# First unit of weights in two halves ahead of attention, next three units two places sooner

## The chip, the core and the metric

The kernel runs on one core of one Trainium2 chip. A time is the device time of one execution in microseconds (us); three executions of the kernel before took 899.27 us in the median (897.33 to 899.37). The engines are TensorE (PE; its weight loads are shown as PEld), VectorE (DVE), ScalarE (ACT), GpSimd (POOL) and SyncE (SP), which here issues nearly all DMA transfers. Each engine runs its own instructions in their order and waits on semaphores for the others.

## What is computed

Local attention with a few global tokens, and a feed-forward network over its output, in 32-bit floats.

```python
def _attn_ref(q_l, k_l, v_l, q_g, k_g, v_g):          # 8 batches, 8 heads, 512 local + 32 global, 64 wide
    s_g = scale * np.matmul(q_g, k_all.transpose(0, 1, 3, 2))      # global queries see all keys
    out_g = np.matmul(sm(s_g), v_all)
    s_ll = np.where(abs(pos[:, None] - pos[None, :]) <= 32, s_ll, -1e9)
    a_l = sm(np.concatenate([s_lg, s_ll], axis=-1))                # local queries: 32 global + a band
    out_l = np.matmul(a_l, np.concatenate([v_g, v_l], axis=2))
    return np.concatenate([out_g, out_l], axis=2)
def _moe_ref(x, w_in, w_out):                          # 4352 tokens, 512 -> 2048 -> 512
    h = x @ w_in
    g = np.where(h > 0.0, h, np.exp(np.minimum(h, 0.0)) - 1.0)
    return g @ w_out
```

The weights w_in and w_out arrive as 64-bit floats.

## The kernel before

Two streams are written into one program. `attention()` yields some hundreds of places; at each place i it writes the pieces that its plan has for that place: loads (k, q, the global queries qg, v), S (scores on PE, masked and reduced on DVE, line 752, exponentials on ACT, line 757), T (turning p, PE line 774, copies to pt on DVE and ACT, line 777), V (product with v, PE line 803, division on DVE, line 817) and X (the output turned to feature-major, xr). A head group g holds four heads; a tile t is 128 local queries. The first pieces, of batch 0 and group 0, are the scores of the global queries (PE line 705, maximum mg on DVE line 708, exponentials on ACT line 711) and the tiles 0 to 3.

`ffn_stream()` is the feed-forward part. It multiplies in 16 bits, each number split into a high and a low half (win and wout "h" and "l"; x likewise), with scales that are powers of two. Its first matmuls are line 316.

Between the two, `load_weights()` makes these halves from the 64-bit weights, in 16 units of 1 MB: unit 0 is the first part of w_in, unit 1 the first of w_out, and so on in turn. `fetch` loads a unit into a tile `raw`, of which there are two; `unit` then defers its steps to later places:

- s0: ACT takes the absolute value of the high word into `cu` (line 178), POOL clamps it (line 179)
- s1m (w_in only): DVE reduces its maximum (line 183)
- s1a, s1b, s1c: DVE shifts the word and merges sign and low bits into it (lines 187, 190, 194), "the words"; after s1c `raw` is free, and SP's next fetch waits for that
- s1d to s4: scales, and the two 16-bit halves (lines 200, 212 and 215)

Up to place 57 (`lead`) no feed-forward work is written, and `UNITS` names the places at which a unit is taken up; each such call fetches one unit ahead and starts the steps of the one before. From place 49 on `convert` paces the units instead. All steps but s0 and s2 are written "behind", with a priority 60 lower. The scheduler that turns this into each engine's order moves rows by these priorities and by its own model of times, so the order of an engine isn't that of the code.

DMA transfers go out in SP's order. A transfer whose buffer is still in use stops SP, with all that stands behind it.

Of the kernel before, what the change touches and what calls it, by code (L numbers as in the profile page):

```python
# [10 lines left out]
F32 = mybir.dt.float32  # L11
F32R = mybir.dt.float32r
I32 = mybir.dt.int32
AF = mybir.ActivationFunctionType
ALU = mybir.AluOpType
AX = mybir.AxisListType
# [6 lines left out]
P = 128  # L23
# [15 lines left out]
NBL = B * SL // BLK  # L39
GROUPS = {"a": (0, 2), "b": (2, 4), "c": (4, 6), "d": (6, 8), "f": (0, 8)}  # L40
BEHIND = 60
UNITS = 0, 7, 17, 28
NX = 4
TURNED = 4

# [5 lines left out]
FMIN = struct.unpack("f", struct.pack("I", 0x38000000))[0]  # L51
FMAX = struct.unpack("f", struct.pack("I", 0x47efe000))[0]
# [5 lines left out]
def attn_ffn(ctx: ExitStack, tc: tile.TileContext, qT, qgT, kT, vT, w_in, w_out, mask, out):  # L58
    nc = tc.nc
# [75 lines left out]
    w1 = w_in.bitcast(I32).rearrange("(c p) (f w) -> p c f w", p=P, w=2)  # L135
    w2 = w_out.bitcast(I32).rearrange("(f p) (e w) -> p f e w", p=P, w=2)
# [10 lines left out]

    def load_weights():
        todo = [(group, m, p) for group in "abcd" for p in range(*GROUPS[group]) for m in range(2)]
        raws = [fetch(*todo[0][1:])]  # L150
        yield
        for n, (group, m, p) in enumerate(todo):
            if n + 1 < len(todo):
                raws.append(fetch(*todo[n + 1][1:]))
            unit(m, p, raws[n])
            if (m, p) == (1, GROUPS[group][1] - 1):
                defer(12, lambda group=group: tables(group))
                if p == NP - 1:
                    defer(13, lambda: tables("f"))
            yield  # L160

    def fetch(m, p):
        raw = ffn.tile([P, NC, 2 * P, 2] if m == 0 else [P, 2, DM, 2], I32, name="raw")
        nc.sync.dma_start(raw, w1[:, :, 2 * p * P:2 * (p + 1) * P, :] if m == 0 else w2[:, 2 * p:2 * p + 2, :, :])
        return raw

    def unit(m, p, raw):
        f = slice(2 * p * P, 2 * (p + 1) * P)
        shape = [P, NC, 2 * P] if m == 0 else [P, 2, DM]
        parts = [w[:, :, f] for w in win] if m == 0 else [w[:, 2 * p:2 * p + 2, :] for w in wout]  # L170
        pw = (pww if m == 0 else pwo)[:, p:p + 1]
        u = ffn.tile(shape, F32, name="cu", bufs=3)
        mx = ffn.tile([P, 4], F32, name="cm", bufs=4)
        high, low = raw[..., 1], raw[..., 0]
        ui = u.bitcast(I32)

        def s0():
            nc.scalar.activation(u, high.bitcast(F32), AF.Abs)
            nc.gpsimd.tensor_scalar(u, u, FMAX, FMIN, ALU.min, ALU.max)

        def s1m():
            if m == 0:
                nc.vector.tensor_reduce(out=mx[:, 0:1], in_=u, op=ALU.max, axis=AX.XY)

        def s1a():
            tc.keep_in_program_order(
                nc.vector.tensor_scalar(ui, ui, 3, 0x3ffffff8, ALU.logical_shift_left, ALU.bitwise_and))

        def s1b():
            nc.vector.scalar_tensor_tensor(out=ui, in0=high, scalar=-0x40000000, in1=ui,  # L190
                                           op0=ALU.bitwise_and, op1=ALU.bitwise_or)

        def s1c():
            nc.vector.scalar_tensor_tensor(out=ui, in0=low, scalar=29, in1=ui,
                                           op0=ALU.logical_shift_right, op1=ALU.bitwise_or)

        def s1d():
            if m:
                dump = ffn.tile([P, 10, P], F32, name="gx", bufs=1)[:, 0:8, :].rearrange("p (a b) x -> p a (b x)", a=2)
                nc.scalar.activation(dump, u, AF.Abs, accum_out=mx[:, 1:2])  # L200

        def s2():
            if m == 0:
                all_max(mx[:, 1:2], mx[:, 0:1])

        def s3():
            if m:
                power(pw, mx[:, 1:2])
            else:
                power_of_wide(pw, mx[:, 1:2], mx[:, 2:3])  # L210
            inverse(mx[:, 3:4], pw)
            nc.scalar.activation(parts[0], u, AF.Copy, scale=mx[:, 3:4])

        def s4():
            nc.vector.scalar_tensor_tensor(out=parts[1].rearrange("p a b -> p (a b)") if m else parts[1],
                                           in0=u.rearrange("p a b -> p (a b)") if m else u, scalar=mx[:, 3:4],
                                           in1=parts[0].rearrange("p a b -> p (a b)") if m else parts[0],
                                           op0=ALU.mult, op1=ALU.subtract)

        d = 1 if lead[0] else 2  # L220
        lag = 7 if m else 13
        for i, fn in ((1, s0), (1 + d, s1m), (1 + d, s1a), (1 + 2 * d, s1b), (1 + 3 * d, s1c), (1 + 4 * d, s1d),
                      (1 + lag, s2), (2 + lag, s3), (3 + lag, s4)):
            defer(i, (lambda fn=fn: behind(fn)) if fn not in (s0, s2) else fn)

    def tables(group):
# [729 lines left out]
    for i, _ in enumerate(attention()):  # L956
        lead[0] = i < PACE[1][0]
        if i in UNITS:
            next(units)
# [70 lines left out]
```

## Time and profile before

| | us |
|---|---|
| median of three executions | 899.27 |
| the profiled execution | 901.09 |
| its span, first to last instruction | 899.0 |
| busy: PE, DVE, ACT, POOL | 859.6, 686.2, 598.8, 85.9 |
| DVE busy from 10.5 to 62 us | 49.60 of 51.50 |
| PE busy from 200 to 899 us | 685.59 of 699 |

All views come from the one profiled execution. Times in them count from its first instruction, and a row of the view in order of time gives start, duration, engine, line, operation, output and inputs, and in brackets how long the engine had been idle and what ended that. "issue" there is idle time for which the profile shows no cause. A row of the waits gives the total, how often, and the longest. The share of DMA is the mean over 16 DMA engines. Neighbouring instructions on DVE overlap by some hundredths of a microsecond, so that their durations add up to a little more than the time they take.

### The profile page before, as it was taken

Reading aid. Unit: us, or ns where it says so; the run is one execution under the profiler, and the core shown is the slowest. Engines: PE = TensorE matmul, PEld = TensorE weight load, DVE = VectorE, ACT = ScalarE, POOL = GpSimd, SP = SyncE. Lnnn points to the kernel's source line nnn. Section 1 sums busy time; section 2 is a strip of 40 time slices with the busy share of each in tenths; the row PEclk is TensorE's granted clock in tenths of the full one; section 3 lists DMA queues with packets and bytes.
Section 4 is the critical chain, followed back from the end, with each engine's and each line's share of the span. In section 5 each row is a group of like instructions: output and inputs, shape, how many; then the busy total and the mean of one; then the engine's idle time right before and its main releaser. Section 6 shows DMA issues by size and latency. Waiting matters only on the chain.

```text
span 899.0 us, 27480 instructions
## 1 busy us (share of the span) xinstructions
PE 859.6 (96%) x11648; PEld 693.1 (77%) x11648; DVE 686.2 (76%) x1910; ACT 598.8 (67%) x1093; POOL 85.9 (10%) x140
## 2 busy tenths in 40 slices
PE   7779999989999999999999999999999999999997
PEld 4557666656656888888878888888888888888886
DVE  5996999989976768776766768686777677766565
ACT  4758987666665656676756667666667666666564
POOL 1110234213210000000000000000000000020000
PEclk7889999999999999999999999999999999999999
DMA  7975756423463335132341335132431211020000
GB/s 284 338 248 179 246 204 223 155 94 111 163 209 133 96 112 160 50 81 66 103 126 47 96 112 160 51 91 85 134 109 57 56 60 47 25 25 24 1 25 24
DMA packets 64818, 103.68 MB, mean 115 GB/s; under 512 B 31288, under 2 KB 31928, under 8 KB 64696
## 3 DMA queue, kind: packets, MB, share of 16 engines
q1 hardware_dynamic: 64408, 101.66, 35.7%
q8 instruction: 92, 1.51, 0.7%
q14 instruction: 30, 0.25, 0.1%
q10 hardware_dynamic: 288, 0.26, 0.1%
HBM read 80.41 MB, written 15.20 MB: 106 GB/s over the span
## 4 chain that ended last, share of the span: by engine, by line
PE 57%; DVE 24%; ACT 13%; issue 3%; DMA 3%; SPq 0%; DVEq 0%; ACTq 0%
PE pa L316 22%; PE acc L474 10%; PE h L474 8%; DVE gl L337 3%; PE acc L439 3%; PE h L316 3%; ACT p L757 3%; ACT gh L353 2%; PE pa L741 2%; PE pa L774 2%; DVE gx L334 2%; PE pa L803 2%; ACT g L325 2%; ACT hs L326 1%; ACT g L327 1%
## 5 line engine op out<-in xcount | busy, mean ns | idle before, releaser
L316 PE MATMUL pa<-x,winh 128*128 128x256 f16 x1648 | 277.5, 273 | 0.6 <-ACT xglob L847 0.6
L316 PEld LDWEIGHTS <-winh 128*128 128x128 f16 x2160 | 208.2, 98 | 36.0 <-issue 4.2
L316 PE MATMUL pa<-x,winl 128*128 128x256 f16 x824 | 224.6, 273 | 0.0
L353 ACT ACTIVATE gh<-gx,xs 128x896 f16<-128x896 f32 x103 | 107.6, 1045 | 142.9 <-DVE gx L350 142.8
L337 DVE SCALAR_TENSOR_TENSOR gl<-gx,xs,gh 128x896 f16<-128x896 f32 x103 | 118.4, 1149 | 76.1 <-ACT gh L353 75.9
L474 PEld LDWEIGHTS <-gh 128*128 128x128 f16 x1456 | 139.8, 98 | 18.8 <-issue 1.4
L334 DVE SCALAR_TENSOR_TENSOR gx<-g,hs 128x512 f32<-128x512 f32 x103 | 71.1, 690 | 76.3 <-ACT g L327 75.6
L316 PEld LDWEIGHTS <-winl 128*128 128x128 f16 x1080 | 105.9, 98 | 12.9 <-issue 0.2
L757 ACT ACTIVATE p<-p,m 128x128 f32<-128x128 f32 x256 | 81.4, 391 | 28.3 <-DVE m L752 28.3
L316 PE MATMUL h<-x,winh 128*128 128x256 f16 x512 | 88.1, 275 | 0.0
L474 PE MATMUL acc<-wouth,gh 128*128 128x256 f16 x312 | 85.2, 273 | 0.0
L474 PE MATMUL acc<-woutl,gh 128*128 128x256 f16 x312 | 85.1, 273 | 0.0
L474 PE MATMUL acc<-wouth,gl 128*128 128x256 f16 x312 | 85.0, 273 | 0.0
L327 ACT ACTIVATE g<-g 128x512 f32<-128x512 f32 x135 | 84.9, 629 | 0.0
L325 ACT ACTIVATE g<-pa,xs 128x512 f32<-128x512 f32 x103 | 70.1, 680 | 17.5 <-PE pa L316 16.6
L474 PEld LDWEIGHTS <-gl 128*128 128x128 f16 x728 | 71.2, 98 | 9.3 <-DVE gl L337 1.0
L474 PE MATMUL h<-raw,gh 128*128 128x256 f16 x416 | 74.6, 273 | 0.0
L587 POOL TENSOR_SCALAR xs<-isc,xm 128x2 f32<-128x2 f32 (+1 forms) x28 | 19.1, 682 | 566.2 <-DVE xm L115 422.3
L316 PE MATMUL h<-x,winl 128*128 128x256 f16 x256 | 70.2, 275 | 0.0
L326 ACT ACTIVATE hs<-pa,xs 128x512 f32<-128x512 f32 x103 | 70.2, 682 | 0.0
L474 PE MATMUL h<-raw,gl 128*128 128x256 f16 x208 | 56.7, 273 | 0.0
L439 PE MATMUL acc<-wouth,gh 128*128 128x512 f16 x128 | 49.1, 384 | 5.2 <-DVE o L447 4.1
(217 smaller groups left out, 1541.8 us busy)
## 6 DMA issues: line engine op xcount, KB each, us to landing
v<-vT SPq DMA_DIRECT2D x64, 520.0 KB, 4.9
k<-kT SPq DMA_DIRECT2D x32, 432.0 KB, 4.9
raw<-w_in SPq DMA_DIRECT2D x8, 1024.0 KB, 5.6
q<-qT SPq DMA_DIRECT2D x32, 256.0 KB, 5.4
raw<-w_out SPq DMA_DIRECT2D x8, 1024.0 KB, 5.7
out<-o SPq DMA_DIRECT2D x32, 256.0 KB, 2.5
od<-o SPq DMA_DIRECT2D x24, 256.0 KB, 2.0
o<-od SPq DMA_DIRECT2D x24, 256.0 KB, 3.1
```

Source lines behind the costliest of these rows:

```text
L316: nc.tensor.matmul(h[:, j, :], wt[:, c, f], xt[:, c, :], start=k == 0, stop=k == 11)
L325: nc.scalar.activation(g, hf, AF.Relu, scale=sc[:, p:p + 1])
L326: nc.scalar.activation(hs, hf, AF.Copy, scale=sc[:, 2 * NP + 1 + p:2 * NP + 2 + p])
L327: nc.scalar.activation(g, g, AF.Exp, scale=-1.0)
L334: nc.vector.scalar_tensor_tensor(out=out, in0=ins[0], scalar=-1.0, in1=ins[1], op0=ALU.add, op1=ALU.max)
L337: nc.vector.scalar_tensor_tensor(out=dst, in0=src, scalar=sg, in1=hi, op0=ALU.mult, op1=ALU.subtract)
L353: nc.scalar.activation(gh, gx, AF.Copy, scale=sg)
L439: nc.tensor.matmul(acc[t], gt[:, s], wt[:, f, :], start=p == first and j == 0 and k == 0, stop=p == last and j == 1 and k == 2)
L474: nc.tensor.matmul(cols, gt, w, start=p == 0 and k == 0, stop=last and k == len(todo) - 1, skip_group_check=True)
L587: nc.gpsimd.tensor_scalar(sc[:, r], isc[:, r], mx[:, 2:3], 1.0, ALU.mult, ALU.mult)
L741: nc.tensor.matmul(sp[r][32 * w:32 * w + 32, at:at + P], q[rows, t * P + 32 * w:t * P + 32 * w + 32], k[rows, o:o + P], start=True, stop=True)
L757: nc.scalar.activation(p[:, i, :], p[:, i, :], AF.Exp, bias=m[:, i:i + 1], scale=-1.0)
```

## The change

`fetch` loads unit 0 by two DMAs of two rows each (of four), and `unit` writes its steps s0 to s1c at once, ahead of attention's first piece and once for each half; one more instruction on DVE takes the larger of the two maxima. The later steps of unit 0 stay at their places. The units 1, 2 and 3 are taken up at the places 5, 15 and 26 instead of 7, 17 and 28, with the fetch of the unit behind each.

```diff
-UNITS = 0, 7, 17, 28
+UNITS = 0, 5, 15, 26
...
-        raws = [fetch(*todo[0][1:])]
+        raws = [fetch(*todo[0][1:], pieces=2)]
+        unit(*todo[0][1:], raws[0], pieces=2)
+        yield
+        raws.append(fetch(*todo[1][1:]))
         yield
         for n, (group, m, p) in enumerate(todo):
+            if n == 0:
+                continue
...
+        n = raw.shape[1] // pieces
+        for i in range(0, raw.shape[1], n):
+            nc.sync.dma_start(raw[:, i:i + n], src[:, i:i + n])
...
+        rows = raw.shape[1] // pieces
+        cut = [slice(i, i + rows) for i in range(0, raw.shape[1], rows)]
+        high, low = ([raw[:, c, :, w] for c in cut] for w in (1, 0))
+        us = [u[:, c] for c in cut]
+        ui = [a.bitcast(I32) for a in us]
+
+        def s0(i=0):
+            nc.scalar.activation(us[i], high[i].bitcast(F32), AF.Abs)
+            nc.gpsimd.tensor_scalar(us[i], us[i], FMAX, FMIN, ALU.min, ALU.max)
...
+        words = (1, s0), (1 + d, s1m), (1 + d, s1a), (1 + 2 * d, s1b), (1 + 3 * d, s1c), (1 + 4 * d, s1d)
+        if pieces > 1:
+            for i in range(pieces):
+                for fn in (s0, s1m, s1a, s1b, s1c):
+                    fn(i)
+            nc.vector.tensor_max(mx[:, 0:1], mx[:, 0:1], mx[:, 2:3])
+            words = ()
+        for i, fn in (*words, (1 + lag, s2), (2 + lag, s3), (3 + lag, s4)):
```

Lines move with it. Of the rows below, before and now: fetch 164, 172; Abs 178, 189; clamp 179, 190; reduction 183, 194; shift 187, 198; merges 190 and 194, 201 and 205; from there on a line number is 17 higher (mg 708, 725; scores 752, 769; exponentials 757, 774; first feed-forward matmul 316, 333).

DVE's order at its start, before (after a memset; ISA is the masked score of a 128x128 piece, or the reading of its maximum m):

```order
L708 TENSOR_REDUCE mg<-pa 128x1
L709 TENSOR_REDUCE mg<-pa 128x1
L183 TENSOR_REDUCE cm<-cu 128x1
L710 TENSOR_SCALAR mg<-mg 128x1
L187 TENSOR_SCALAR cu<-cu 128x1024
L752 ISA p,m<-acc,msk 128x128
L752 ISA m 128x1
```

and in the change:

```order
L725 TENSOR_REDUCE mg<-pa 128x1
L194 TENSOR_REDUCE cm<-cu 128x1 x2
L198 TENSOR_SCALAR cu<-cu 128x512 x2
L201 SCALAR_TENSOR_TENSOR cu<-raw,cu 128x512 x2
L205 SCALAR_TENSOR_TENSOR cu<-raw,cu 128x512 x2
L238 TENSOR_TENSOR cm<-cm 128x1
L726 TENSOR_REDUCE mg<-pa 128x1
L769 ISA p,m<-acc,msk 128x128
L769 ISA m 128x1
L727 TENSOR_SCALAR mg<-mg 128x1
```

The words of unit 0 have moved ahead of the first masked scores, and stand behind the first reduction of mg. Unit 1's shift and merges follow after the four masked scores of tile 0; before, they stood after those of tile 2, with the first pt copy among them.

ACT's order at its start, before (pgt is the turned exponentials of the global queries):

```order
L178 ACTIVATE cu<-raw 128x1024
L711 ACTIVATE pg<-pa,mg 128x8x64
L712 ACTIVATE pg<-pa,mg 128x32
L757 ACTIVATE p<-p,m 128x128 x4
L723 COPY pgt<-pa 128x384 x2
L178 ACTIVATE cu<-raw 128x1024
L757 ACTIVATE p<-p,m 128x128 x8
L777 COPY pt<-pa 128x8x64
```

and in the change:

```order
L189 ACTIVATE cu<-raw 128x512 x2
L189 ACTIVATE cu<-raw 128x1024
L728 ACTIVATE pg<-pa,mg 128x8x64
L729 ACTIVATE pg<-pa,mg 128x32
L774 ACTIVATE p<-p,m 128x128 x4
L740 COPY pgt<-pa 128x384 x2
L189 ACTIVATE cu<-raw 128x1024
L774 ACTIVATE p<-p,m 128x128 x8
L794 COPY pt<-pa 128x8x64
```

Before, the Abs ahead of the eight exponentials (tiles 1 and 2) was unit 1's; now it is unit 2's.

SP's order where unit 5's weights are fetched, before (the numbers tell buffers apart; raw_1170 is unit 5, raw_1361 unit 6):

```order
L690 DMA v_792<-vT 128x1040
L690 DMA v_794<-vT 128x1040
L690 DMA v_954<-vT 128x1040
L690 DMA v_956<-vT 128x1040
L164 DMA raw_1170<-w_out 128x2x1024
L690 DMA v_1002<-vT 128x1040
```

and in the change (raw_1178 is unit 5):

```order
L707 DMA v_800<-vT 128x1040
L707 DMA v_802<-vT 128x1040
L172 DMA raw_1178<-w_out 128x2x1024
L707 DMA v_962<-vT 128x1040
L707 DMA v_964<-vT 128x1040
L707 DMA v_1010<-vT 128x1040
```

The fetch of unit 5 stands two loads of v sooner, and on ACT its Abs now stands ahead of the copy of xr and the first split of x (line 565), behind which it stood. From DVE's row 184 on, and at about the same time on the other engines, the orders are the same as before.

More of the change, by code (lines that the diff above doesn't have):

```diff
@@ L160, in load_weights, with fetch, unit @@
             yield
-    def fetch(m, p):
+    def fetch(m, p, pieces=1):
         raw = ffn.tile([P, NC, 2 * P, 2] if m == 0 else [P, 2, DM, 2], I32, name="raw")
-        nc.sync.dma_start(raw, w1[:, :, 2 * p * P:2 * (p + 1) * P, :] if m == 0 else w2[:, 2 * p:2 * p + 2, :, :])
+        src = w1[:, :, 2 * p * P:2 * (p + 1) * P, :] if m == 0 else w2[:, 2 * p:2 * p + 2, :, :]
+        n = raw.shape[1] // pieces
+        for i in range(0, raw.shape[1], n):
+            nc.sync.dma_start(raw[:, i:i + n], src[:, i:i + n])
         return raw
-    def unit(m, p, raw):
+    def unit(m, p, raw, pieces=1):
         f = slice(2 * p * P, 2 * (p + 1) * P)
@@ L173, in unit, with s1m, s1a, s1b @@
         mx = ffn.tile([P, 4], F32, name="cm", bufs=4)
[L174 to L181, printed above, removed]
+        rows = raw.shape[1] // pieces
[6 more added lines that the diff above has]
+            nc.gpsimd.tensor_scalar(us[i], us[i], FMAX, FMIN, ALU.min, ALU.max)
+        def s1m(i=0):
             if m == 0:
-                nc.vector.tensor_reduce(out=mx[:, 0:1], in_=u, op=ALU.max, axis=AX.XY)
-        def s1a():
+                nc.vector.tensor_reduce(out=mx[:, 2 * i:2 * i + 1], in_=us[i], op=ALU.max, axis=AX.XY)
+        def s1a(i=0):
             tc.keep_in_program_order(
-                nc.vector.tensor_scalar(ui, ui, 3, 0x3ffffff8, ALU.logical_shift_left, ALU.bitwise_and))
-        def s1b():
-            nc.vector.scalar_tensor_tensor(out=ui, in0=high, scalar=-0x40000000, in1=ui,
+                nc.vector.tensor_scalar(ui[i], ui[i], 3, 0x3ffffff8, ALU.logical_shift_left, ALU.bitwise_and))
+        def s1b(i=0):
+            nc.vector.scalar_tensor_tensor(out=ui[i], in0=high[i], scalar=-0x40000000, in1=ui[i],
                                            op0=ALU.bitwise_and, op1=ALU.bitwise_or)
-        def s1c():
-            nc.vector.scalar_tensor_tensor(out=ui, in0=low, scalar=29, in1=ui,
+        def s1c(i=0):
+            nc.vector.scalar_tensor_tensor(out=ui[i], in0=low[i], scalar=29, in1=ui[i],
                                            op0=ALU.logical_shift_right, op1=ALU.bitwise_or)
@@ L221, in unit @@
         lag = 7 if m else 13
-        for i, fn in ((1, s0), (1 + d, s1m), (1 + d, s1a), (1 + 2 * d, s1b), (1 + 3 * d, s1c), (1 + 4 * d, s1d),
-                      (1 + lag, s2), (2 + lag, s3), (3 + lag, s4)):
+        words = (1, s0), (1 + d, s1m), (1 + d, s1a), (1 + 2 * d, s1b), (1 + 3 * d, s1c), (1 + 4 * d, s1d)
[6 more added lines that the diff above has]
+        for i, fn in (*words, (1 + lag, s2), (2 + lag, s3), (3 + lag, s4)):
             defer(i, (lambda fn=fn: behind(fn)) if fn not in (s0, s2) else fn)
```

## The prediction

> **What bounds the kernel now.** I read the busy time by stretches first, then VectorE's (DVE) waits up to 66 us, then the start in order of time.
>
> ```profile
> core 0: us, PE busy (x) PEld busy (x) DVE busy (x) ACT busy (x) POOL busy (x), PEclk, DMA share, GB/s
> 0.00:10.50 10.50, 6.98 (x42) 2.49 (x50) 0.27 (x1) 2.40 (x2) 2.51 (x8) 0.89 0.83 292
> 10.50:62.00 51.50, 40.34 (x936) 28.38 (x931) 49.60 (x180) 35.00 (x78) 6.98 (x8) 0.79 0.82 296
> 62.00:78.90 16.90, 13.97 (x298) 10.55 (x279) 10.16 (x40) 11.33 (x22) 3.10 (x6) 0.90 0.44 139
> 200.00:899.00 699.00, 685.59 (x9219) 576.39 (x9216) 511.64 (x1414) 452.65 (x822) 38.70 (x69) 1.00 0.29 85
> ...
> DVE mg L708 <- PE pa L705: 9.4, 1, 9.4
> DVE pt L777 <- PE pa L774: 1.1, 2, 0.7
> DVE p L752 <- PE pa L741: 0.8, 1, 0.8
> DVE xm L851 <- ACT xr L841: 0.3, 1, 0.3
> DVE sm L814 <- PE h L810: 0.2, 1, 0.2
> ```
>
> Three stages. Until 10.5 us DVE has nothing to do (0.27 us busy). From 10.5 to 62 it is busy 49.60 of 51.50 us, and its waits there are 1.1 + 0.3 + 0.2 = 1.6 us (the 0.8 lies at 65.8): DVE bounds this stage. After it TensorE (PE) takes over, 685.59 of the last 699 us. As the instructions from row 184 of DVE's order on stand as before, I take it that a shift at about 66 us, where the first block of the feed-forward part starts, travels to the end unchanged. So the question is what happens to those first 66 us.
>
> ```profile
> 6.29 1.12 ACT L178 ACTIVATE cu<-raw 128x1024 f32<-128x1024 f32 x1 [4.28 <-DMA raw<-w_in]
> 7.50 1.04 POOL L179 TENSOR_SCALAR cu<-cu 128x1024 f32<-128x1024 f32 x1 [5.47 <-ACT cu L178]
> 7.65 2.03 PE L705 MATMUL pa<-k,qg 64*32 64x512 f32 x10 [2.33 <-DMA k<-kT]
> 10.58 0.69 DVE L708 TENSOR_REDUCE mg<-pa 128x1 f32<-128x512 f32 x1 [9.45 <-PE pa L705]
> 11.28 1.21 DVE L183 TENSOR_REDUCE cm<-cu 128x1 f32<-128x1024 f32 x1
> 12.53 0.69 DVE L187 TENSOR_SCALAR cu<-cu 128x1024 int32<-128x1024 int32 x1
> 13.98 1.26 DVE L190 SCALAR_TENSOR_TENSOR cu<-raw,cu 128x1024 int32<-128x1024 int32 x1
> 15.27 1.22 DVE L194 SCALAR_TENSOR_TENSOR cu<-raw,cu 128x1024 int32<-128x1024 int32 x1
> 16.58 0.38 SPq L164 DMA_DIRECT2D raw<-w_in  x1
> 16.74 2.45 ACT L757 ACTIVATE p<-p,m 128x128 f32<-128x128 f32 x8 [0.18 <-DVE m L752]
> 19.69 0.69 DVE L777 COPY pt<-pa 128x512 f32<-128x512 f32 x1 [0.70 <-PE pa L774]
> 20.29 1.22 DVE L190 SCALAR_TENSOR_TENSOR cu<-raw,cu 128x1024 int32<-128x1024 int32 x1
> 21.64 1.27 DVE L194 SCALAR_TENSOR_TENSOR cu<-raw,cu 128x1024 int32<-128x1024 int32 x1
> 22.24 1.18 ACT L178 ACTIVATE cu<-raw 128x1024 f32<-128x1024 f32 x1
> ```
>
> **1. The words ahead of attention: nothing gained.** On DVE the first unit costs 1.21 + 0.69 + 1.26 + 1.22 = 4.38 us, in the full stage. Done in the empty stretch before 10.58 it would save that. The data would allow it: the whole unit is clamped by 7.50 + 1.04 = 8.54 us now, and the second half can hardly be later. But the order of the change puts the first maximum of attention's scores, L725 (L708 before), in front of the first reduction L194, and that row waits for PE until 10.58. DVE runs its rows in order, so all of unit 0's words still lie behind 10.58. I take 0; the other end is -4.38.
>
> **2. Two halves.** Twice a 128x512 reduction (0.69, L708) against 1.21 is +0.17 in durations. For the two word merges the nearest row is a 128x512 instruction of their kind:
>
> ```profile
> 76.11 0.69 DVE L334 SCALAR_TENSOR_TENSOR g<-g,hs 128x512 f32<-128x512 f32 x1 [2.50 <-ACT g L327]
> ```
>
> 2 x (2 x 0.69) against 1.26 + 1.22 is +0.28. The shift (0.69 whole) and the added maximum have no row of their size; for both I take 0.05 (between 0 and 0.69 + 0.21, if a half cost as much as a whole). Sum +0.5. The second weight DMA takes about 0.46 us of SP ahead of the loads of q and k; the DMA engines are 0.83 busy until 10.5 us and k comes behind the same megabyte, so I take 0 for it (between 0 and 0.46).
>
> **3. ACT's queue waits for weights where it ran the softmax.** The buffer of unit 0 is free once its last merge has ended: now 15.27 + 1.22 = 16.49, and SP fetches unit 2 at 16.58. In the change 10.58 + 0.69 + 4.38 + 0.5 = 16.15 us, so the fetch is sooner by some 0.4 us. Now it lands after 5.6 us; the second row spans all weight transfers of the first 120 us:
>
> ```profile
> raw<-w_in SPq DMA_DIRECT2D x1, 1024.0 KB, 5.6
> DMA to landing us min/median/max: 4.8/6.0/9.0
> ```
>
> That gives 21.8 us. Before, ACT's Abs for unit 2 (22.24) stood behind the eight exponentials of the second and third tile (16.74 to 19.19). In the change it stands before them, and ACT runs its rows in order. So they start at 21.8 + 1.18 = 22.9; the first four (half of 2.45) end at 24.2, PE turns them in the 0.5 us that lay between 19.19 and 19.69, and DVE's copy of pt starts at 24.7. DVE would be there at 19.69 - 0.70 + 0.5, plus unit 1's two merges, which now stand ahead of the copy (1.22 + 1.27): 22.0. It waits 2.7 us instead of 0.70: +2.0. Bounds: +1.2 with a transfer of 4.8 us and +5.4 with one of 9.0. Behind the Abs stand the exponentials, and behind those the copies that PE's product with v waits for.
>
> **4. Clamps beside merges.** Where GpSimd's clamp ran beside a merge, the merge grew:
>
> ```profile
> 33.55 1.04 POOL L179 TENSOR_SCALAR cu<-cu 128x1024 f32<-128x1024 f32 x1 [9.02 <-ACT cu L178]
> 33.71 1.96 DVE L194 SCALAR_TENSOR_TENSOR cu<-raw,cu 128x1024 int32<-128x1024 int32 x1
> 23.50 1.04 POOL L179 TENSOR_SCALAR cu<-cu 128x1024 f32<-128x1024 f32 x1 [5.81 <-ACT cu L178]
> 23.64 0.91 DVE L121 SCALAR_TENSOR_TENSOR pww<-cm 128x1 int32<-128x1 int32 x1
> ```
>
> 1.96 against 1.22 is 0.74. In the change unit 1's clamp comes at about 14 to 15 us, on unit 0's merges, and unit 5's at about 60, on unit 4's: +1.4. The clamp that held the tiny L121 at 23.6 (0.91, some 0.75 too long) now falls into DVE's wait of part 3: -0.75. Sum +0.65 (part 3 is not touched by it: the fetch follows the last merge, and so does DVE), between -0.75 and +1.5. The Trainium skill, page "SBUF — State Buffer", section "Who interferes with whom", says that a DVE instruction with two SBUF inputs and a GpSimd instruction that reads SBUF exclude each other for the whole instruction; by it each new clash could cost up to the clamp's 1.04, and the sum would be +1.3. The trace agrees in kind (1.96 and 0.91).
>
> **5. The later units.** Their DVE work is the same and lies in the same full stage; of the waits that it still holds, 0.4 us (the second pt copy) is there to be filled: -0.4. What does move is unit 5's transfer, from behind four loads of v to behind two, which went out at 44.93:
>
> ```profile
> 44.93 1.64 SPq L690 DMA_DIRECT2D v<-vT  x2
> 55.49 0.38 SPq L164 DMA_DIRECT2D raw<-w_out  x1
> 52.00:54.00 2.00, 2.00 (x65) 1.77 (x68) 2.00 (x18) 2.00 (x7) 0.00 (x0) 0.50 0.00 0
> 64.55 1.17 ACT L178 ACTIVATE cu<-raw 128x1024 f32<-128x1024 f32 x1 [3.05 <-DMA raw<-w_out]
> 64.93 0.86 PE L741 MATMUL pa<-k,q 64*32 64x128 f32 x39 [2.42 <-issue]
> q8 instruction: 1, 0.02, 3.8%
> 65.72 0.39 PE L316 MATMUL h<-x,winh 128*128 128x256 f16 x2
> ```
>
> Before, the transfer went out at 55.49 and held ACT until 64.55. At 62.5 PE stops for 2.42 us and waits for nothing that the profile shows; the one 16 KB transfer of instructions (q8; 0.02 MB) between 58 and 64 us lies in the answer for 62.4 to 64. I read the stall as PE's own instructions, late behind unit 5's megabyte and the v's. In the change the transfer goes out once unit 3's last merge has freed the buffer. That merge, now at 43.86, takes 1.87:
>
> ```profile
> 43.86 1.87 DVE L194 SCALAR_TENSOR_TENSOR cu<-raw,cu 128x1024 int32<-128x1024 int32 x1
> ```
>
> With 2.75 of lateness (parts 2 to 5) that is 48.5, some 7 us sooner than 55.49, so it fills the time at 52 to 54 in which the DMA engines move nothing (share 0.00). I take the stall as gone, -2.4 (between 0 and -2.42). ACT now has unit 5's Abs (1.18) before the copy of xr and the split of x; DVE, which uses them, is 2.75 late and covers it. Without that cover it is +1.2.
>
> **The sum.** 0 + 0.5 + 2.0 + 0.65 - 0.4 - 2.4 = +0.35 us, made against the profiled execution: span 899.0 becomes 899.35, its time 901.09 becomes 901.4. The median of the three runs shown is 1.8 us under that execution, 899.27; with the same 0.35 the forecast is 899.6. Less than about 0.3%, 2.7 us, a measurement of this kernel can't tell from no change: faster is under 896.6, slower over 902.0.
>
> **Rivals.**
>
> *A. PE's stall stays.* Without the -2.4 the time is 899.27 + 2.75 = 902.0, at the edge of slower. For it: no row shows what PE waited for. Against it: the busy DMA engines and the instruction transfer inside the stall. The Trainium skill, page "Runtime: NRT & Kernel Launch", section "Instruction fetch mechanics", says that a sequencer fetches its next 16 KiB while it executes the current block, so that the cost of crossing is mostly hidden; by that rule late instructions are no cause, and this rival holds. The transfer inside the stall (0.02 MB) speaks for an exception here. Chance 0.20.
>
> *B. Slower: ACT's wait for unit 2's weights grows.* One place, the Abs ahead of the exponentials of tiles 2 and 3; each us by which the transfer lands after 21.8 us is one us on DVE. From 24.2 on (2.35 more) the change is slower. With 9.0 us it costs 5.4 in place of 2.0: 899.6 + 3.4 = 903.0. For it: one weight transfer took 9.0, and v, k and q follow this one at once. Against: the same unit landed in 5.6 with the k's behind it. Chance 0.13.
>
> *C. Faster: the weights' earlier arrival outweighs the rest.* ACT's wait of 3.05 before 64.55 goes too, and the exponentials of the global scores behind it, and PE's turns of them, come earlier. With the lower ends of parts 3 and 4 (1.2 and -0.75): 0.5 + 1.2 - 0.75 - 0.4 - 2.4 = -1.85, and half of 3.05 more, -3.4: 895.9. For it: PE is the bound from 62 to 78.9 (13.97 of 16.90 in spite of the stall). Against: DVE still has to come first. Chance 0.20.
>
> *D. Faster: the words do fill the empty stretch.* Part 1 at its other end, and no wait in part 3, since the fetch of unit 2 would go out 4.4 us sooner: 899.6 - 4.38 - 2.0 = 893.2. It needs DVE to pass the row that waits for PE, against its order. Chance 0.05.
>
> **How the numbers follow.** The forecast has the remaining 0.42. Of it I put 0.34 within 0.3% and 0.04 on each side; A gives 0.10 to same and 0.10 to slower, B 0.04 and 0.09, C 0.07 to same and 0.13 to faster, D 0.05 to faster. That makes 0.22 faster, 0.55 same, 0.23 slower. The likeliest case's own range, 897.5 to 902.0, comes from the bounds of part 4 and a stall that goes in part. The whole range takes in C's 895.9 and B's 903.0 and leaves out D and the worst of A and B together: 895.8 to 903.0.
>
> **What would show it.** Right: L725 still starts DVE at about 10.6 us with the word rows behind it; the Abs of unit 2 starts at about 22 us with ACT idle before it and "DMA raw" as what ended that; the second pt copy follows a DVE wait of some 2.7 us; no PE gap over 1 us between 60 and 67; the first matmul of the feed-forward part (L333, L316 before, at 65.72) starts at 66.1 within 1.5 us; every later row is moved by the same amount. Wrong: DVE working at 8 us; the pt copy without a wait; the first feed-forward matmul before 63 or after 69; or a shift there that doesn't reach the end, which would mean that the stages after 66 us are bound by something that doesn't move with them.

## The result: slower by 0.9%

| | before | after |
|---|---|---|
| median of five executions, us | 899.27 | 906.67 |
| lowest to highest | 897.33 to 899.61 | 905.61 to 908.49 |
| the profiled execution, its span | 901.09, 899.0 | 905.93, 903.9 |

The ratio is 1.0089, with a 95% interval of 1.0074 to 1.0104: the change costs 6.7 to 9.4 us. The forecast was 899.6 us, and 906.67 lies above its range. One execution of a later kernel, e9, ran at a mean granted clock of 0.746 and took 1102.84 us; it is left out of every ratio and median here.

The profiled execution of the changed kernel is 4.9 us longer in its span. That is less than the some 8 us of the ratio: the one of before (901.09) is slower than the five others of its kernel, and the one of the change (905.93) the second fastest of five, so this pair shows little more than half of the loss. Nearly all of what it shows has come about by the first matmul of the feed-forward part, and it stays to the end. The first rows are of the kernel before, in order of time (the first feed-forward matmul, and a row near the end):

```profile
65.72 0.39 PE L316 MATMUL h<-x,winh 128*128 128x256 f16 x2
...
889.41 0.40 ACT L383 ACTIVATE gh<-g,xs 128x128 f16<-128x128 f32 x1 [1.64 <-DVE g L401]
```

and the same rows of the changed kernel:

```profile
70.39 0.38 PE L333 MATMUL h<-x,winh 128*128 128x256 f16 x2 [0.69 <-DVE tok L834]
...
894.11 0.40 ACT L400 ACTIVATE gh<-g,xs 128x128 f16<-128x128 f32 x1 [1.64 <-DVE g L418]
```

That is 4.67 us at the first row and 4.70 at the second. Where they come from is seen in the busy time by stretches, of the kernel before:

```profile
10.50:20.00 9.50, 7.25 (x137) 4.83 (x132) 8.69 (x34) 6.55 (x18) 1.04 (x1) 0.68 0.69 244
20.00:30.00 10.00, 7.39 (x178) 4.70 (x161) 10.00 (x29) 6.55 (x11) 1.04 (x1) 0.84 1.04 405
30.00:42.00 12.00, 10.00 (x221) 7.16 (x221) 11.37 (x45) 8.58 (x23) 1.04 (x1) 0.77 0.87 315
```

and of the changed one (columns as in the prediction's first view: length, then busy us of PE, PEld, DVE, ACT and POOL, PE's granted clock, DMA share, GB/s):

```profile
10.50:20.00 9.50, 3.75 (x58) 2.36 (x62) 9.30 (x23) 3.80 (x9) 2.03 (x1) 0.68 0.65 233
20.00:30.00 10.00, 8.33 (x203) 4.99 (x190) 8.73 (x40) 8.72 (x19) 1.04 (x1) 0.89 1.03 401
30.00:42.00 12.00, 9.73 (x145) 6.88 (x146) 6.89 (x22) 4.75 (x10) 2.04 (x1) 0.60 0.74 271
```

From 10.5 to 20 us DVE works a little more than before, but PE falls from 7.25 to 3.75 us and ACT from 6.55 to 3.80. Later, from 30 to 42, DVE itself falls from 11.37 to 6.89. The start in order of time shows the first of the two. Before, the second maximum of mg and the exponentials that need it:

```profile
11.19 0.18 DVE L709 TENSOR_REDUCE mg<-pa 128x1 f32<-128x32 f32 x1
12.73 0.69 ACT L711 ACTIVATE pg<-pa,mg 128x512 f32<-128x512 f32 x1 [5.33 <-DVE mg L710]
```

and in the change:

```profile
10.63 0.69 DVE L725 TENSOR_REDUCE mg<-pa 128x1 f32<-128x512 f32 x1 [9.50 <-PE pa L722]
11.24 1.27 DVE L194 TENSOR_REDUCE cm<-cu 128x1 f32<-128x512 f32 x2
...
14.48 2.03 POOL L190 TENSOR_SCALAR cu<-cu 128x1024 f32<-128x1024 f32 x1 [7.05 <-ACT cu L189]
15.51 1.01 DVE L238 TENSOR_TENSOR cm<-cm 128x1 f32<-128x1 f32 x1
16.44 0.18 DVE L726 TENSOR_REDUCE mg<-pa 128x1 f32<-128x32 f32 x1
17.07 0.69 ACT L728 ACTIVATE pg<-pa,mg 128x512 f32<-128x512 f32 x1 [2.67 <-DVE mg L727]
17.30 1.09 PE L758 MATMUL acc<-k,q 64*32 64x128 f32 x14 [5.75 <-DVE m L769]
...
21.01 1.13 ACT L189 ACTIVATE cu<-raw 128x1024 f32<-128x1024 f32 x1 [0.63 <-DMA raw<-w_in]
...
23.95 0.69 DVE L794 COPY pt<-pa 128x512 f32<-128x512 f32 x1 [0.98 <-PE pa L791]
```

The second maximum of mg now starts at 16.44 us, where it started at 11.19. Everything that needs the first maxima is late with it: ACT's first exponentials start at 17.07 (12.73 before), PE stands 5.75 us, and the first copy of the turned scores starts at 23.95 (19.69 before). The loss is already 4.3 us at that row.

The second shows in DVE's waits. Up to 65 us DVE waited 1.6 us before. Now it waits for PE's products and turns:

```profile
DVE pt L794 <- PE pa L791: 2.8, 4, 1.3
DVE sm L831 <- PE h L820: 2.8, 2, 2.3
DVE p L769 <- PE acc L758: 0.9, 1, 0.9
```

Two things stand beside these waits. The weight work that lay among attention's rows there before has already been done: unit 2's merges, winl and woutl end by 32.6 us, before the first tok. And PE itself is slower there. The first row is of the kernel before, the second of the change:

```profile
36.00:42.00 6.00, 5.17 (x123) 3.12 (x120) 5.49 (x30) 4.30 (x14) 0.00 (x0) 1.00 0.87 296
36.00:42.00 6.00, 6.00 (x114) 4.70 (x114) 2.21 (x12) 2.44 (x8) 0.00 (x0) 0.50 0.56 219
```

In the change PE is busy for all of these 6 us, at half its clock, and DVE waits for it. How much of the second loss comes from the order and how much from the clock, this pair doesn't tell.

### The profile page after: what moved, and what is told of

It reads as the page before. It is cut to its first block, busy times and chain, and to the rows that moved or that the text cites. A ratio compares the mean times of both kernels' runs of the same rounds, so it can differ in the third digit from the quotient of the medians.

```text
span 903.9 us, 27486 instructions
## 1 busy us (share of the span) xinstructions
PE 858.9 (95%) x11648; PEld 692.4 (77%) x11648; DVE 686.7 (76%) x1915; ACT 597.7 (66%) x1094; POOL 91.2 (10%) x141
## 4 chain that ended last, share of the span: by engine, by line
PE 54%; DVE 27%; ACT 12%; DMA 4%; issue 2%; SPq 0%; DVEq 0%; ACTq 0%
PE pa L333 22%; PE acc L491 10%; PE h L491 8%; DVE gl L354 4%; ACT gh L370 2%; DMA raw<-w_in 2%; ACT p L774 2%; PE pa L791 2%; DVE gx L351 2%; PE pa L758 2%; PE acc L456 2%; PE pa L820 2%; ACT g L342 2%; PE h L333 2%; DVE cu L201 2%
## 5 line engine op out<-in xcount | busy, mean ns | idle before, releaser
L604 POOL TENSOR_SCALAR xs<-isc,xm 128x2 f32<-128x2 f32 (+1 forms) x28 | 21.3, 762 | 551.7 <-DVE xm L115 411.6
```

The costliest lines, as they stand in the source:

```text
L604: nc.gpsimd.tensor_scalar(sc[:, r], isc[:, r], mx[:, 2:3], 1.0, ALU.mult, ALU.mult)
```

## The experiments

All runs are compared with runs of the kernel before on the same chip; since its median there goes from 897.56 to 900.04 us, ratios are the better measure. 0.0010 is 0.9 us. A profile is one execution, and the places where PE's clock falls to half differ between executions: its mean over the first 66 us is 0.82 in the profile of before, 0.77 in the change's, and 0.74 (e10) to 0.87 (e8) in those of the table below. So times read from the profiles are less sure than the ratios. Unit 1 of the weights is the first of w_out; unit 2, the second of w_in, is the one whose Abs the prediction's part 3 speaks of.

### The places alone, and the early words alone

e1 is the kernel before with the new places, e2 the changed kernel with the old ones.

```diff
e1:  -UNITS = 0, 7, 17, 28      (kernel before)
     +UNITS = 0, 5, 15, 26
e2:  -UNITS = 0, 5, 15, 26      (changed kernel)
     +UNITS = 0, 7, 17, 28
```

> The kernel before with only the places of the units changed (0, 5, 15, 26); unit 0 is fetched whole and its words are written at their old places. Theory order (the loss comes from DVE's order between 26 and 33 us: in the changed kernel five rows of weight work, 4.9 us, stand ahead of the first division of attention's output, tok, for which PE waits; the stretch from 30 to 42 us then loses some 4.5 us of DVE's work): here DVE's order has tok ahead of winl, woutl and unit 2's merges, so the loss is small, 899 to 901 us. Theory early words (the words of unit 0 ahead of the first masked scores, with the clamp that collides with them and the Abs that waits, set everything back): 898 to 900 us. Theory places (the weight transfers that go out sooner push q back, for which PE waited 1.74 us): 903 to 906 us.

> The changed kernel with the old places of the units (0, 7, 17, 28): unit 0 in two halves and its words early, the rest as before. Theory order: DVE's order has the first tok ahead of winl and woutl and the second behind them, and unit 2's merges after the second copy of pt, nearly as before; it keeps the some 2 us that the changed kernel had lost by 25 us and little more, 900 to 902 us. Theory early words: all of the loss, 905 to 907 us. Theory places: none of it, 898 to 900 us.

Measured: e1 902.04 us, ratio 1.0031 (1.0016 to 1.0045); e2 905.14, 1.0061 (1.0038 to 1.0085). The larger part belongs to the early words, and within the intervals the two add up (0.0031 + 0.0061 against 0.0089). In e2's profile the first copy of the turned scores starts at 25.27 us, so the late start of attention comes with the words. e1's profiled execution was the second shortest of its ten (900.29, span 897.8), with PE at its full clock until 23.5 us, and shows its first copy at 18.94 and its first feed-forward matmul at 65.08, no later than before. Its second copy of pt on DVE starts at 33.00 us, 31.35 before, with both merges of unit 2 now ahead of it. Whether e1's 2.8 us come from that can't be read from this execution; the cause of the places' part stays open.

### Is it the weight work ahead of tok?

In the trace of the changed kernel four weight rows of DVE (woutl, winl and both merges of unit 2) stand between the sums of the softmax and the first tok, and PE waits for that tok. e3 holds them behind the first two tok.

```diff
+            if fn in (s1b, s1c, s4) and 15 <= now[0] + i <= 19:
+                held.add(fn)                  # pinned in written order
+                i = 20 - now[0]
```

> The changed kernel with one thing moved: the five rows of weight work (winl, woutl, both merges of unit 2, among them) are held behind the first two tok on DVE. Theory order: the wait of DVE between 33 and 42 us (5.1 us in the changed kernel) shrinks to 1 to 2 us, and the time falls by 3 to 4 us to 902 to 904 us. Theory early words: what was lost by 25 us stays, and nothing is gained after it, 905 to 907 us. Theory places: PE still waits for q, 905 to 907 us.

Measured: 903.72, 1.0062 (1.0039 to 1.0085). The time lies in the range of the theory of order, though its interval overlaps that of the change, and DVE's idle time from 33 to 42 us went from 5.1 to 0.45, as that theory expected. But the path got no shorter in the profile: the first tok started at 32.89 us, against 32.56, since the product with v was late itself, and the first feed-forward matmul at 72.02, against 70.39. So the rows ahead of tok aren't what makes the first tok late, and that lateness lies before them. A small share of the loss, up to 0.0027 by the two ratios, may still lie in them; the intervals can't tell.

### The words put into the empty stretch

e4 makes the words of unit 0 do what the change's place for them suggests: the two first maxima are pinned behind them, so that DVE works before 10.5 us.

```diff
+            def pinned(top):
+                return tc.keep_in_program_order(top) if np_[0] == 0 else top
-            nc.vector.tensor_reduce(out=m[:, 0:1], in_=sp[0], op=ALU.max, axis=AX.X)
+            pinned(nc.vector.tensor_reduce(out=m[:, 0:1], in_=sp[0], op=ALU.max, axis=AX.X))
```

> The changed kernel with the first two reductions of mg held behind unit 0's words on DVE, so that the words run before 10.6 us, in the stretch in which DVE has nothing to do. All theories have DVE at work from about 6 us, and mg at about 11 us. Theory early words: the cause of the loss is gone and some 4 us of DVE's work with it, 896 to 900 us. Theory order: the five rows still stand ahead of tok, 4 us sooner; 902 to 904 us. Theory places: 902 to 904 us.

Measured: 906.46, 1.0079 (1.0053 to 1.0105). No theory had expected that. DVE did 3.7 us of the words before 10.5, and then stood at the next unit's row, ahead of tile 1's scores:

```profile
DVE cu L198 <- POOL cu L190: 2.9, 1, 2.9
```

Unit 1's transfer had landed only at 13.9 us (ACT's Abs starts there after 7.12 us of idle time), its clamp came behind that, and its shift stands on DVE ahead of tile 1. So e5 also takes unit 1's words off that place, with the old places, and e6 does this one thing alone to the changed kernel.

```diff
e5, e6:
+            if (m, p) == (1, 0) and fn is not s0:
+                i = max(i, {s1m: 14, s1a: 14, s1b: 14, s1c: 15, s1d: 15, s2: 16, s3: 16, s4: 17}[fn] - now[0])
e5 besides: the pinned maxima of e4, and UNITS = 0, 7, 17, 28
```

> The changed kernel with three edits: the first piece's two maxima are held behind the words of unit 0, as in e4_words_first; the later units go back to their old places (0, 7, 17, 28); and the words of unit 1 (its shift and its two merges on DVE) are held until the masked scores of tiles 1 and 2 are written, where the kernel before has them. Theory 'latency chain' (what counts is how much weight work stands on DVE ahead of the masked scores of tiles 0 to 2; the rest of the loss follows from that): only some 0.5 to 1 us of unit 0's words are left ahead of tile 0, so the first turned copy comes at 19 to 20 us (before 19.69, after 23.95) and the time is 897 to 900. Theory 'missing filler' (the early words are gone from the later waits of DVE, so the loss comes wherever unit 1 stands): first turned copy near 20, but DVE idles 3 us or more between 30 and 42 us, and the time is 902 to 905. Theory 'halves cost' (the two halves, two transfers and the clamp beside DVE's merges, cost the 6 us of e2 by themselves): 904 to 906.

> The changed kernel with one edit: the words of unit 1 on DVE, some 3 us, are held until the masked scores of tiles 1 and 2 are written; places (0, 5, 15, 26) and the words of unit 0 in two halves ahead of tile 0's scores are as in the change. Latency chain: the first turned copy comes 2 to 3 us sooner than the 23.95 of the change, at 21 to 22, and the time is 902 to 904.5. Missing filler or halves cost: 905 to 907, as the change.

Measured: e5 906.63, 1.0100 (1.0082 to 1.0118); e6 910.96, 1.0135 (1.0100 to 1.0170), the slowest of all. Both lie above every range that was expected. The theory in its first form, that what counts is the weight work on DVE ahead of the first scores, falls: e5 has next to none there. In e6 DVE now simply waits where the weight rows stood:

```profile
22.05 0.29 DVE L771 CUSTOM_DVE_ANT_0 p<-pa,msk 128x128 f32<-128x128 f32 x1 [3.42 <-PE pa L760]
...
26.43 0.29 DVE L771 CUSTOM_DVE_ANT_0 p<-pa,msk 128x128 f32<-128x128 f32 x1 [2.40 <-PE pa L760]
26.65 0.69 DVE L796 COPY pt<-pa 128x512 f32<-128x512 f32 x1
```

The first copy of the turned scores starts at 26.65, 2.7 us later than in the change, behind one masked score of tile 3 that the scheduler has now put ahead of it and that waited 2.40. The weight rows of unit 1 had cost nothing there; they lay under waits.

e5's trace shows what had been missed:

```profile
12.13 0.28 DVE L774 CUSTOM_DVE_ANT_0 p<-acc,msk 128x128 f32<-128x128 f32 x1
...
13.82 1.12 ACT L189 ACTIVATE cu<-raw 128x1024 f32<-128x1024 f32 x1 [7.13 <-DMA raw<-w_out]
14.84 0.68 ACT L733 ACTIVATE pg<-pa,mg 128x512 f32<-128x512 f32 x1
...
15.84 1.51 PE L744 MATMUL pa<-ident,pg 128*128 128x128 f32 x6 [2.15 <-ACT pg L734]
...
18.48 0.29 DVE L774 CUSTOM_DVE_ANT_0 p<-pa,msk 128x128 f32<-128x128 f32 x1 [5.31 <-PE pa L763]
...
23.75 1.91 PE L724 MATMUL pa<-k,qg 64*32 64x512 f32 x2
25.60 1.62 PE L825 MATMUL h<-v,pt 128*32 128x65 f32 x50
```

DVE had its first maxima by 12.5 us. ACT, though, stood at the Abs of unit 1 until that unit's transfer landed at 13.82, with the first exponentials behind it; PE's turns waited for those, tile 1's scores stood behind the turns, and DVE waited 5.31 us for them. A second moved row is on PE: two score matmuls of the second group, which the kernel before has behind the product with v, now stand inside it (23.75), and the product ends late. PE ran at half its clock there, from 15.0 to 28.6 us, which made both longer. Three in-order queues had been changed, and only one of them had been put back.

### The same words, behind tile 0's scores

e7 fetches, makes absolute and clamps unit 0 in halves at the start, with the old places, but its DVE rows are written behind tile 0's masked scores.

```diff
-                for fn in (s0, s1m, s1a, s1b, s1c):
-                    fn(i)
+                s0(i)
...
+            words = ((6, later_words),)       # the rest of both halves
```

> The changed kernel with the old places (0, 7, 17, 28), and with unit 0 still fetched, made absolute and clamped in two halves at the start, but the DVE work of its words (two maxima, two shifts, four merges) written down behind tile 0's masked scores, about where the kernel before has it. Compared with e2_halves_only (905.14) only where DVE does that work differs. Latency chain: first turned copy within 1 us of the kernel before (19 to 21), time 898.5 to 901. Halves cost: 904 to 906 as e2.

Measured: 902.45, 1.0053 (1.0036 to 1.0069), between the two expectations. The first copy starts at 20.68 us, about where it should, and the rest is lost later. The largest place in sight is of the same kind: at 48 to 52 us weight rows of later units stand between the sums and the tok for which PE waits, 4.13 us against 1.6 before. That this is the rest was not tested.

```profile
48.19 0.14 DVE L834 TENSOR_SCALAR sm<-h 128x4 f32<-128x4 f32 x1
48.26 1.20 DVE L194 TENSOR_REDUCE cm<-cu 128x1 f32<-128x1024 f32 x1
49.41 1.28 DVE L226 SCALAR_TENSOR_TENSOR winl<-cu,cm,winh 128x1024 f16<-128x1024 f32 x1
50.67 0.15 DVE L834 TENSOR_SCALAR sm<-h 128x4 f32<-128x4 f32 x1
...
51.48 0.75 DVE L837 TENSOR_TENSOR tok<-h,sm 128x256 f32<-128x256 f32 x2
...
52.05 1.14 PE L860 MATMUL pa<-ident,tok 128*128 128x128 f32 x4 [4.13 <-DVE tok L837]
```

### All three queues put back, and each by itself

e8 is e5 with ACT's and PE's moved rows pinned to the order of the kernel before; e10 has only ACT's, e11 only PE's; e12 is e8 without the pinned maxima, so that the words stand behind the first maximum, as in the change.

```diff
e8, e10, e12 (ACT: Abs of units 1 and 2 in written order, unit 1's from place 9 on):
+            if (m, p) in ((1, 0), (0, 1)):
+                tc.keep_in_program_order(top)
e8, e11, e12 (PE: scores of tile 2, and of the second group's global queries):
+                            if (st["b"], g, t) == (0, 0, 2):
+                                tc.keep_in_program_order(top)
+                        if st["b"] == 0 and g == 1:
+                            tc.keep_in_program_order(top)
```

> As e5_words_first_unit1_held (words of unit 0 in DVE's empty stretch before 10.6 us, old places, words of unit 1 held behind the masked scores of tiles 1 and 2), and besides the rows of the other two queues that e5 left moved are put back where the kernel before has them: on ACT the Abs of unit 1 behind tile 0's exponentials (in e5 ACT stood 7.13 us on unit 1's transfer until 13.82, with the first exponentials behind it until 14.84; before they start at 12.73) and the Abs of unit 2 behind the first copy of the turned scores; on PE all of tile 2's scores behind the turns of pg, and the second group's 16 score matmuls behind V. Theory 'queue heads' (the loss of the change is what its moved rows stand ahead of on ACT and PE as much as on DVE: an in-order queue whose head waits for something late): first turned copy by 20.5 us, first tok by 27, first FFN matmul by 66.5, time 895 to 900. Theory 'missing filler' (DVE's early words are missing from its later waits, whatever stands where): as e5, 904 to 907. Theory 'clock' (PE's share of busy time in the first 20 us is what counts, since a 3.4 us window with little work is followed by one at half clock): 899 to 903, by how long the half-clock stretches are.

> e5_words_first_unit1_held with only ACT's rows put back (Abs of unit 1 behind tile 0's exponentials, Abs of unit 2 behind the first copy of the turned scores); the scores on PE are held nowhere, and two of tile 2's score matmuls still stand ahead of the turns of pg (with ACT's rows back, the 16 turns of the scores stand in one piece again, and the second group's score matmuls behind V). If ACT's queue head (7.13 us on unit 1's transfer, with tile 0's exponentials behind it) is the larger part of the 7 us between e5 and e8: first turned copy by 20, 898.5 to 902. If it is PE's rows: 903.5 to 907.

> e5_words_first_unit1_held with only PE's rows put back (tile 2's scores behind the turns of pg, the second group's score matmuls behind V); ACT still has the Abs of units 1 and 2 ahead, as in e5. If ACT's queue head is the larger part: first turned copy at 21 to 22.5, 903 to 906. If PE's rows are: 898.5 to 902.

> e8_all_queues_back with one edit: the first piece's two maxima are no longer held behind the words of unit 0, so that these stand where the change has them, behind the first maximum, 4.3 us on DVE between that maximum at 10.6 us and tile 0's masked scores; ACT, PE and unit 1 as in e8. Theory 'queue heads': all that waits for the first maxima (first exponentials, turns, V) comes some 4 us later than in e8: first turned copy at 22 to 23.5 instead of 18.61, first FFN matmul at 67.5 to 69.5 instead of 64.83, time 902.5 to 905. If only ACT's and PE's moved rows cost: 898.5 to 901.5.

| run | us | ratio (95%) | first pt copy | first feed-forward matmul |
|---|---|---|---|---|
| e5, DVE alone put right | 906.63 | 1.0100 (1.0082 to 1.0118) | 22.25 | 73.01 |
| e8, all three | 899.50 | 1.0007 (0.9988 to 1.0026) | 18.61 | 64.83 |
| e10, DVE and ACT | 900.62 | 1.0008 (0.9989 to 1.0027) | 19.78 | 67.97 |
| e11, DVE and PE | 901.51 | 1.0017 (1.0000 to 1.0034) | 20.82 | 67.58 |
| e12, as e8 but words as in the change | 904.77 | 1.0059 (1.0036 to 1.0082) | 23.06 | 68.83 |

e8 gives back the whole loss, as the theory of queue heads expected, in all four numbers. e12's order on DVE differs from e8's by the place of one row, the first maximum, which stands ahead of unit 0's words in e12 and behind them in e8; ACT's, POOL's and SP's orders are the same. e12 lands in all three of its expected ranges: 0.0052 in the ratio, 4.7 us, give or take some 0.003, and the two intervals don't meet. Its start, against e8's, is the cleanest picture of the cause. e12:

```profile
11.51 0.69 DVE L731 TENSOR_REDUCE mg<-pa 128x1 f32<-128x512 f32 x1 [10.38 <-PE pa L726]
...
16.45 0.19 DVE L732 TENSOR_REDUCE mg<-pa 128x1 f32<-128x32 f32 x1
17.18 0.67 ACT L734 ACTIVATE pg<-pa,mg 128x512 f32<-128x512 f32 x1
18.17 1.51 PE L745 MATMUL pa<-ident,pg 128*128 128x128 f32 x6 [5.75 <-ACT pg L735]
20.82 0.29 DVE L778 CUSTOM_DVE_ANT_0 p<-pa,msk 128x128 f32<-128x128 f32 x1 [3.22 <-PE pa L764]
```

e8:

```profile
11.99 0.18 DVE L735 TENSOR_REDUCE mg<-pa 128x1 f32<-128x32 f32 x1
...
13.00 0.67 ACT L737 ACTIVATE pg<-pa,mg 128x512 f32<-128x512 f32 x1
...
13.99 1.51 PE L748 MATMUL pa<-ident,pg 128*128 128x128 f32 x6 [1.70 <-ACT pg L738]
...
16.63 0.29 DVE L781 CUSTOM_DVE_ANT_0 p<-pa,msk 128x128 f32<-128x128 f32 x1 [3.22 <-PE pa L767]
```

From the second maximum to tile 1's first score it takes 4.37 us in e12 and 4.64 in e8, through ACT and PE, and DVE waits 3.22 us at its end in both: the weight work ahead of the maximum moves the whole chain, and fills none of its waits. PE's clock has no part in the shift of that maximum: in e12 it stands behind 4.3 us of words on DVE. By the first feed-forward matmul the two profiles are 4.0 us apart. Their spans are 7.6 apart, so that e12's execution, one of the slowest of its eight, lost more behind that point, where the orders don't differ.

e10 and e11 miss as a pair: one of them should have shown the larger part, and each gave back nearly all of it. ACT's and PE's moved rows cost 0.001 or less singly, within the intervals, and 0.0093 together, 8.4 us (e5 against e8). In e11 ACT still stood until 13.94 us, but with the turns and the product with v in one piece on PE the first copy starts at 20.82 us, 1.4 sooner than in e5, and the first tok at 28.14, 2.9 sooner. And with ACT's rows back alone, the scheduler puts PE's second-group scores behind the product by itself, so that e10 isn't ACT's order alone. How much belongs to either is open.

By ratios the change can be put together: 0.0007 (e8) for the halves and the new order with all heads put right, 0.0052 for the words behind the first maximum (e12 less e8), 0.0031 for the places (e1): 0.0090, against 0.0089 measured. Each term is known to some 0.002 or 0.003, so an agreement that close is chance. As far as the intervals tell, the ACT and PE rows and unit 1's rows add nothing in the change itself: e2, which has them moved, and e12, which has them back, stand at 1.0061 and 1.0059. A likely reason, not tested, is that behind a start that is late by 4.3 us on DVE, ACT and PE would have waited anyway.

### Is it PE's clock?

PE is granted half its clock in the changed kernel from 15.4 to 22.2 us. e9 gives it something to do before: 16 matmuls of zeros, which nothing reads, behind tile 0's scores.

```diff
+    def fill():
+        for _ in range(16):
+            tc.keep_in_program_order(nc.tensor.matmul(..., warm[:, 0:P], warm, start=True, stop=True))
+    defer(7, fill)
```

> The changed kernel with 16 matmuls of zeros more on PE (128x512, like the ten at the start; nothing reads them), behind tile 0's scores, where PE otherwise stands idle from 11.2 to 17.3 us. Theory 'clock': PE's granted clock in the changed kernel is 0.5 from 15.4 to 22.2 us because the window before (12.0 to 15.4) had no work; with that window filled the clock from 15.4 on is 1.0, the first turned copy comes 1 to 2 us sooner than at 23.95, and the time is 903.5 to 905.5. Theory 'queue heads': the chain waits for DVE and ACT, the clock costs nothing that they do not hide: 906 to 908.

Measured: 905.41 in the median of three, 1.0077 (1.0053 to 1.0101), no better than the change as far as the intervals tell; the time alone doesn't decide between the theories. By stretches, the changed kernel:

```profile
12.00:15.40 3.40, 0.00 (x0) 0.00 (x0) 3.40 (x7) 1.20 (x1) 0.92 (x1) 1.00 0.46 187
15.40:18.80 3.40, 1.50 (x16) 0.90 (x17) 3.37 (x14) 1.73 (x6) 1.11 (x1) 0.50 0.54 137
```

and e9:

```profile
11.80:15.20 3.40, 3.40 (x16) 1.36 (x16) 3.40 (x8) 1.16 (x1) 0.65 (x1) 1.00 0.50 205
15.20:18.60 3.40, 1.31 (x35) 0.91 (x35) 3.37 (x15) 1.31 (x4) 1.53 (x1) 1.00 0.46 94
18.60:22.00 3.40, 3.40 (x48) 2.46 (x48) 2.08 (x10) 2.29 (x8) 0.00 (x0) 0.50 1.04 406
```

The clock did stay at 1.00 from 15.2 to 18.6, and the first copy started at 24.01 us, where it was 23.95, not 1 to 2 us sooner: PE waited for DVE until 17.43 all the same. So the half clock doesn't cause the late start. The test isn't clean, for the scheduler moved rows here too: unit 1's last merge (22.88 us) now stands directly ahead of that copy, and PE's last turn ended at 23.43, so that without the merge the copy could have come some 0.5 us sooner, by an estimate from these rows. The half clock came 3.4 us later instead, and what it costs over the whole of the first 70 us hasn't been measured.

## Why the prediction was wrong, step by step

**What bounds the kernel.** This is the step that failed: "DVE bounds this stage" was read from 49.60 busy us in 51.50, and from it followed that DVE's work moved within the stage costs nothing. The share was right, the conclusion wasn't: DVE was full because weight rows lay in the waits of a chain that goes from DVE's maxima over ACT's exponentials and PE's turns and products back to DVE. e8 does 3.9 us of the words before 10.5 us, DVE's busy time from 10.5 to 62 us falls from 49.60 to 43.68, and the time stays the same (1.0007, 0.9988 to 1.0026). Where DVE did not wait before, e8 has a wait of 3.2 us:

```profile
DVE p L781 <- PE pa L767: 3.2, 1, 3.2
```

**Part 1** was right as to where the words land (L725 starts at 10.63, the words behind it) and wrong as to what that costs. It took 0, since the same work moved within a full stage. It measured +4.7 (e12 against e8), because the words went ahead of the second maximum and of the first masked scores, for which ACT and PE wait. DVE's order, as shown with the change, has them there. Neither end of its bounds, 0 and -4.38, has that sign.

**Part 2**, +0.5, was about right for the words: their rows add up to 4.60 us in place of 4.38, and the added maximum takes 0.15 where no clamp lies beside it (e12). For the second DMA it took 0, and that was too little. PE's first matmul behind the k's starts at 7.65 and 7.67 us in the two profiles without halves (before, e1). In the twelve with them it starts at 7.67 to 9.47, in the middle at 8.5, some 0.8 later; the change's own profile has the earliest of the twelve. SP issues the k's 0.48 later (2.27 against 1.79 us); what makes the rest is open. e8 has this lateness too (8.43) and still loses nothing in sum.

**Part 3** had the mechanism in its rows, but not the path. The Abs of unit 2 does stand ahead of the exponentials and waits for its transfer, only for 0.63 us, and DVE waits 0.98 us for the first copy, not 2.7. The lateness had arisen on DVE before that. That the copy starts at 23.95 us, where 24.7 was forecast, is chance. And the forecast had charged only half of it: from 19.69 to 24.7 is 5.0 us, of which parts 2 and 3 counted 0.5 and 2.0; the other 2.5, unit 1's merges ahead of the copy, went for nothing, as work moved within a full stage. The measured copy is 4.26 late, and the first feed-forward matmul 4.67.

**Part 4**, +0.65, was right in kind and about right in size: POOL's clamp at 14.48 takes 2.03 us, and the added maximum of two numbers beside it 1.01 (0.15 in e8, where no clamp lies beside it); the merge beside unit 5's clamp at 64 us takes 1.94, and L121 falls from 0.91 to 0.15. The Trainium skill's page "SBUF — State Buffer", section "Who interferes with whom", has DVE and POOL exclude each other in such pairs; these rows agree.

**Part 5** says the failed step once more: the later units' "DVE work is the same and lies in the same full stage", priced at -0.4. With the places alone, e1 is 0.0031 slower, 2.8 us, from a cause that is open. DVE's busy time from 30 to 42 us fell by 4.5 us, and its waits up to 65 us, 1.6 before, have 6.5 in the three rows shown. The same work in another order isn't the same time where the order decides what the other engines wait for. The other half of part 5 came out: PE's stall of 2.42 us before the feed-forward part is gone (its longest wait from 60 to 67 us is 1.1, for tok), and the gain is contained in the 4.67 that are left.

**That a shift at 66 us reaches the end unchanged** was right for this pair: 4.67 and 4.70. It doesn't hold to the microsecond: over all fourteen profiles the time from the first feed-forward matmul to the end goes from 831.7 (e2, e7) to 837.1 us (e12), 833.3 before.

**The rivals.** A (the stall stays) didn't happen. B had the right sign and nearly the right row: an Abs that waits for its transfer ahead of exponentials. In the change itself it cost 0.63 us, on unit 2; in e5 the same thing on unit 1 held ACT's first exponentials until 14.84 us, 1.84 later than in e8. C did not happen. D, the words in the empty stretch, was priced at 893.2; e8 made it so and gave 899.5. The 4.38 us that it expected was DVE's busy time, which isn't the path's; the later arrival of the k's may hide a gain of under 1 us.

## What to carry to other kernels

An engine that is busy nearly all the time need not be the bound: work of low urgency can fill the waits of a chain over several engines, and the share of busy time then looks the same as that of a bottleneck. Before counting moved work at nothing, follow the first links of each chain and list, for every in-order queue, what now stands ahead of each link, and when that row's input arrives; a row in front of a link can cost its whole length plus its wait, as the words did here. After moving work by places or priorities, compare the order of all engines: here a change on DVE and SP also moved Abs rows on ACT and scores on PE, and putting back DVE alone (e5) gained nothing.

## What the hardware showed that was not expected

PE's granted clock in the first 70 us goes between 1.0 and 0.5 in windows of 3.4 us, whose places differ from one execution to the next. In the fourteen profiles of this case, cut at those windows up to 72 us, each of the 47 windows at full clock in which PE's records cover 48% or less was followed by one at half clock, and of the more than fifty with 75% or more all but one by one at full clock; between these it went either way. From half clock back to full it never went after a window with less than 73%. The rows of e9 above show both: 3.40 of 3.40 us keeps the clock, 1.31 of 3.40 loses it. The Trainium skill's page "TensorE: Matmul & The Clock Gate", section "What's actually happening", has the half clock follow an idle window of about 3.4 us, with windows that run free of the kernel; the traces agree with the length and the free phase, and show besides that a window needn't be idle for it. So a late chain can make PE slower too, by windows that the kernel doesn't set. That may be part of why executions of one kernel differ by up to 7.4 us (e6: 905.05 to 912.46). The granted clock of every execution speaks for it: in most of these kernels the longer executions tend to have the lower mean clock (e8: 897.94 us at 0.988, 905.10 at 0.982; e6: 905.05 at 0.986, 912.46 at 0.975). Which of the two causes the other, these numbers don't show.
